# A short table for v in PSUM, one reciprocal per half batch, two batches' hypermixer in one pass, more buffers and a new order

## The chip, the cores and the metric

The kernel runs on one core of one Trainium2 chip. The metric is the device time of one launch in microseconds (us). TensorE is called PE in the profile (PEld is its weight load), VectorE DVE, ScalarE ACT, GpSimd POOL, SyncE SP; SP issues all transfers. A core has 16 DMA engines.

## What is computed

Linear attention with cosine weights, then a token mixer, over 8 batches of 576 tokens, 8 heads of 64:

```python
r = relu(x);  phi(x) = concat([r * cos_w, r * sin_w], -1)    # cos_w, sin_w: one number per position
kv  = einsum('bhsf,bhsd->bhfd', phi(k), v);  z = sum(phi(k), axis=2)
x   = (phi(q) @ kv) / (phi(q) . z + 1e-6)                    # heads side by side: [8, 576, 512]
wq, wk = x @ w_q, x @ w_k                                    # 64 columns each
mixed  = (wq @ wk^T / 8) @ x                                 # over the tokens of one batch
out    = relu(mixed) @ w_out                                 # [8, 576, 512] float32
```

q, k and v are float32 in HBM, 9.4 MB each; out is 9.4 MB. The kernel works in bfloat16 and sums in float32.

## The kernel before, in words

The work is cut into 16 half batches H (four heads each, two pairs of heads side by side in the 128 partitions), 8 batches b, and for the last product 36 row tiles of 128 tokens. Every piece of work is a *step*, a small Python function that issues the instructions of one piece. The string `ORDER` (L24) names all steps with their index, the PSUM bank or bank pair that they write (`:4`) and the engine (`@A` ACT, `@V` DVE, `@G` POOL). The loop at L434 issues them in just this order, so each engine's program is `ORDER` cut to its steps. No scheduler moves anything; an engine waits at its next instruction until the operands are there and the buffer is free.

The steps of one half batch:

- `LK LQ LV` (L129) load k, q, v: two DMAs of 288 KB each, on SP's queue, into raw buffers (`NRAW` = 4 per tensor).
- `RK`, `RQ` (relu, L201, L204) and `CV` (a cast of v, L208) make bfloat16 of them, on ACT or POOL.
- `VS` (L211, DVE) multiplies v by cosine and by sine of the position. The table `vtab` (L137) holds both for each of 9 positions, repeated 64 times along the head's columns: 1152 bfloat16 a partition in SBUF.
- `QT` (L239, PE) transposes q in 18 small transposes; `QM` (L252, DVE) multiplies the result, out of PSUM, by `qtab`.
- `KV` (L227, PE) makes kv and z in 36 matmuls; `KE` (L248) copies them to SBUF.
- `N` (L261, PE), twice per half batch (index g = 2H + r): 20 matmuls that make numerator and denominator.
- `EP` (L274, ACT or DVE) adds eps to 10 denominators a partition; `X` (L281, DVE) takes their reciprocal (L286) and multiplies 640 numerators a partition by it (L287). Both once per g, so 32 times.
- `XT` or `XR` (L292, L303, PE) transpose x; `XE` copies that to SBUF.

Then for each batch: `WK KW WQ QW` (wk, wq and their copies out of PSUM), `KX XK` (wk^T x), `XA XB` (copy halves of it across partitions), four `MX` (two matmuls each, L378) with `ME` (relu, L388); and for two batches at a time nine row tiles `WO` (four matmuls of 512 columns, L398), `OE` (copy) and `ST` (store, L412), out of `NOUT` = 12 output buffers. PSUM has eight banks of 2 KB a partition; `pair(i)` is banks i and i + 1. `make_identity`, iotas (`TK`, `TQ`) and ACT's `Sin` (`TV`, `TW`, `T2`) make identity and tables at the start; `LW`, `CW` load and cast the weights.

Of the kernel before, what the change touches and what calls it, by code (L numbers as in the profile page):

```python
# [24 lines left out]
LV1 LQ0b LQ1 TK CV1@G TQ LK1 TV LV0a TI TZ LV0b T2 RK1@G RQ1@A TW VS1 LK0a CV0b@A QT1:0 RQ0b@A  # L25
LQ0a CV0a@G KV1:2 LK0b RK0a@G RQ0a@A QM1 KE1@V RK0b@A VS0a VS0b N2:4 LV3 LQ3 RQ3@A LK3 CV3@G EP2@V
N3:6 LV2 LK2 QT0:0 KV0:2 X2 EP3@A LQ2 RK3@G QM0 KE0@A VS3 N0:4 LV5 X3 QT3:0 EP0@A KV3:2 QM3 LW0
LW1 X0 CV2@G KE3@A RK2@A VS2 XT1:6 N1:0 EP1@A LK5 LQ4 X1 N6:4 CV5@G LQ5 XE1@A RQ2@A EP6@A LV7 N7:2
LV4 KV2:0 QT2:6 EP7@A LQ7 KE2@V XT0:0 X6 CW1 QM2 CW0 N5:4 XE0@A WK0:6 N4:0 RK5@A X7 RQ5@G WQ0:7
VS5 EP4@V X4 EP5@V KW0@A RQ4@A KX0:6 XR3:2 XK0@A QW0@V X5 XB0@A XE3@A XA0@A KV5:0 LK4 LQ6 KE5@A  # L30
QT5:6 LW2 XT2:4 CV7@G MX1:2 QM5 LV6 XE2@A MX3:0 QT4:6 CV4@G ME1@A ME3@A RK4@G MX2:4 VS4 LK7 QM4
WK1:2 WQ1:3 KW1@A N11:0 RQ7@G KX1:2 CW3@G N10:6 QW1@V ME2@A MX0:4 XK1@A EP11@A ME0@A VS7 X11 KV4:2
EP10@A KE4@A N9:4 X10 N8:0 RQ6@A CW4@G XT5:2 EP8@A X8 LV8 LK6 CV6@G RK7@G QT7:6 LV10 CW2@A EP9@A
X9 XA1@A CW5@A WO1:0 XE5@A LQ8 LV9 XR4:4 QT6:2 WO2:1 QM7 OE1:0@A KV7:6 XB1@G QM6 RK6@G VS6 XE4@A
MX7:2 WQ2:0 KE7@A MX4:4 ME7@A OE2:1@A N15:6 MX5:2 QW2@A ME4@V EP15@A WK2:1 N14:4 LK10 ME5@A KW2@A
KV6:2 EP14@A X15 CV8@G KE6@A MX6:0 ME6@A KX2:6 LQ9 X14 N12:2 VS8 LK8 XK2@A EP12@A N13:0 EP13@A X13
# [12 lines left out]
WK5:5 ME19@A X24 MX18:0 N27:6 XR12:2 OE14:8@A KW5@A ST5 ME18@A VS15 RQ15@G EP27@A RK15@G N26:4
KX5:0 XK5@A EP26@V WO18:1 WO16:0 X27 X26 QT15:6 QT14:4 XE12@A OE16:7@A XR13:2 WO20:0 OE18:6@A ST8  # L50
RK14@G VS14 XE13@A QM14 WO19:1 QM15 ST7 WK6:2 OE20:5@A XB5@A KV15:4 XA5@G KW6@A KV14:6 ST20 MX23:2
OE19:4@V KE15@A MX21:0 ST0 WQ6:4 ME21@A KE14@V KX6:5 ME23@V MX20:0 N30:6 MX22:2 QW6@V WO21:4
ME20@A N29:0 EP30@V ST2 ME22@A XK6@A N28:2 X30 N31:6 EP29@A EP28@A X29 X28 OE21:11@A ST12 XB6@A
WO24:5 XA6@G WO22:4 OE24:2@A WO23:5 EP31@A X31 OE22:5@A XR14:0 XR15:2 XE14@A MX27:6 OE23:3@V
WO25:4 ST18 XE15@V ST16 WK7:5 ME27@V OE25:1@A MX26:0 KW7@A ME26@A MX25:2 ST14 MX24:6 WQ7:4 KX7:5
ME24@V ME25@A WO26:0 XK7@A QW7@V XB7@A WO29:1 MX31:6 XA7@G ST22 MX28:2 ME31@A ST9 MX30:4 OE26:10@V
WO28:0 ST21 MX29:6 ST23 ST1 ME30@A OE29:6@V WO30:1 ST25 ME29@A ST19 ME28@V ST29 OE28:7@V WO32:0
ST24 WO31:4 ST26 ST28 WO33:5 OE32:8@V OE30:5@A ST32 ST30 OE31:9@A ST31 OE33:11@A WO27:6 OE27:3@A
ST33 WO35:7 ST27 OE35:0@A ST35 WO34:2 OE34:1@A ST34
# [4 lines left out]
def kernel(  # L64
# [29 lines left out]
    NRAW, NPREP, NV2, NQM, NX, NXT, NOUT = (4, 2, 2, 2, 2, 2, 12)  # L94
# [41 lines left out]
    qi = pool.tile([P, 2, C, H2], I32, name="qi")  # L136
    vtab = pool.tile([P, C, 2, D], BF16, name="vtab")  # L137
# [5 lines left out]
    wo_f = pool.tile([P, NDM, DM], FP32, name="wof")  # L143
    wqw = pool.tile([P, NDM, DH], BF16, name="wqw")
# [8 lines left out]

    def TV(i, ps, eng):
        nc.scalar.activation(vtab, ki.unsqueeze(3).to_broadcast([P, C, 2, D]),
                             AF.Sin, bias=0.0, scale=coef)

# [10 lines left out]
    def T2(i, ps, eng):  # L168
        for b in v2_b:
            for pr in range(2):  # L170
                nc.scalar.activation(b[:, pr, :, :, D:DV],
                                     ki.unsqueeze(3).to_broadcast([P, C, 2, 2]),
                                     AF.Sin, bias=0.0, scale=coef)

    def TZ(i, ps, eng):
        for b in qm_b:
            nc.gpsimd.memset(b[:, :, :, C, :], 0.0)
        for b in xT_b:
            nc.gpsimd.memset(b[:, :, C, :], 0.0)
        nc.gpsimd.memset(eps_t, EPS)  # L180
# [30 lines left out]
    def VS(H, ps, eng, part):  # L211
        n = part.stop - part.start
        V.tensor_mul(  # L213
            v2_b[H % NV2][:, part, :, :, 0:D],
            vb_b[H % NPREP][:, part].unsqueeze(3).to_broadcast([P, n, C, 2, D]),
            vtab.unsqueeze(1).to_broadcast([P, n, C, 2, D]))
# [22 lines left out]
    def QT(H, ps, eng):  # L239
        place["QT", H] = ps  # L240
        qt_v = qt_view(ps)
        for c in range(C):
            for r in range(2):
                a = slice(H2 * r, H2 * r + H2)
                nc.tensor.transpose(qt_v[:, r, c * H2:(c + 1) * H2],  # L245
                                    rq_b[H % NPREP][a, c, :, :], ident[a, a])

    def KE(H, ps, eng):  # L248
        cast(eng, kv_b[H % 2][:, :, :, 0:D + 1],
             kv_view(place["KV", H]).rearrange("p r (s e) -> p r s e", s=2))  # L250

    def QM(H, ps, eng):  # L252
        V.tensor_mul(  # L253
            qm_b[H % NQM][:, :, :, 0:C, :].rearrange("p s r c d -> p s r (c d)"),
            qt_view(place["QT", H]).unsqueeze(1).to_broadcast([P, 2, 2, S]),
            qtab.rearrange("p s c d -> p s (c d)").unsqueeze(2).to_broadcast([P, 2, 2, S]))
# [4 lines left out]
    def N(g, ps, eng):  # L261
# [3 lines left out]
        for u in range(SC):  # L265
            for s in range(2):
                for pr in range(2):
                    a = slice(H2 * pr, H2 * pr + H2)
                    nc.tensor.matmul(  # L269
                        nv[:, pr, u, :], qm_b[H % NQM][a, s, r, 2 * u:2 * u + 2, :],  # L270
                        kv_b[H % 2][a, r, s, 0:D + 1],
                        start=(u == 0 and s == 0), stop=(u == SC - 1 and s == 1))

    def EP(g, ps, eng):  # L274
        den = num(place["N", g])[:, :, :, D:D + 1]
        if eng is A:
            A.activation(rec_b[g % 8], den, AF.Identity, bias=eps_t)  # L277
        else:
            V.tensor_scalar(rec_b[g % 8], den, EPS, None, op0=ALU.add)

    def X(g, ps, eng):  # L281
        H, r = divmod(g, 2)
        b, h = divmod(H, 2)
        rec = rec_b[g % 8]
        nv = num(place["N", g])
        V.reciprocal(rec, rec)  # L286
# [3 lines left out]
            nv[:, :, :, 0:D], rec.to_broadcast([P, 2, SC, D]), op=ALU.mult)  # L290
# [46 lines left out]
    def KW(b, ps, eng):  # L337
        cast(eng, wk_b[b % 2], bank(place["WK", b])[:, 0:SC * DH].rearrange(
# [15 lines left out]

    def KX(b, ps, eng):
        place["KX", b] = ps
        o = bank(ps)
        for u in range(SC):
            for t in range(2):
                nc.tensor.matmul(  # L360
                    o[H2 * t:H2 * t + H2, 0:XC], wk_b[b % 2][:, u, :],
# [15 lines left out]

    def MX(i, ps, eng):  # L378
# [9 lines left out]
    def ME(i, ps, eng):  # L388
# [4 lines left out]
        if eng is A:  # L393
            A.activation(dst, s, AF.Relu, scale=scale_moe)  # L394
        else:
            V.tensor_scalar(dst, s, scale_moe, 0.0, op0=ALU.mult, op1=ALU.max)
# [18 lines left out]
    def LW(i, ps, eng):  # L415
# [14 lines left out]
    steps = {f.__name__: f for f in (KV, QT, KE, QM, N, EP, X, XT, XR, XE, WK, KW, WQ, QW, KX, XK, XA, XB,  # L430
                                     MX, ME, WO, OE, ST, LW, CW, TK, TV, TI, TQ, TW, T2, TZ)}
# [46 lines left out]
```

## Time and profile before

| what | value |
|---|---|
| median of 3 runs | 123.55 us (123.04 to 128.03) |
| span of the profiled execution, first to last instruction | 120.7 us; the median is 2.85 us longer, what lies around the span |
| busy | PE 94.8, DVE 88.2, ACT 84.2, POOL 52.2 us |
| moved | 39.40 MB, mean 326 GB/s; read 29.62 MB, written 9.44 MB |
| granted TensorE clock | 0.991 |

The page's chart cuts the span in 40 slices of 3 us; a digit is the busy share in tenths. The *windows* view gives each engine's busy time in a stretch. The *groups* list instructions of one line with their mean duration; the *timeline* gives start and duration of single ones, with the idle time before and what ended it in brackets. In the *chain of waits* a line is start, duration and what ran; a row there is the time from one group's turn to the next one's, so it leaves out the overlap that a duration of the groups holds.

### The profile page before, as it was taken

What the parts mean: (1) busy time and instruction counts of PE and PEld (TensorE: products, weight loads), DVE (VectorE), ACT (ScalarE), POOL (GpSimd) and SP (SyncE); (2) the same over time, 40 slices, a digit from 0 to 9 for tenths busy, and PEclk for the clock granted to TensorE, in tenths of its full rate; (3) what the DMA queues carried; (4) which work ended last, traced back from release to release, by engine and by line L of the source; (5) the groups of instructions that cost most, each with busy time, mean ns of one, the idle gap of its engine ahead of it and who ended that gap; (6) DMA issues with size and microseconds to landing.
All of it is one profiled execution on the core that took longest, in us unless ns stands there. A gap on an engine that the chain in (4) does not pass through costs nothing.

```text
span 120.7 us, 5301 instructions
## 1 busy us (share of the span) xinstructions
PE 94.8 (79%) x2286; PEld 63.1 (52%) x2286; DVE 88.2 (73%) x132; ACT 84.2 (70%) x155; POOL 52.2 (43%) x63
## 2 busy tenths in 40 slices
PE   0005919758778899969999999798999999999950
PEld 0004818637656656635667576454755864653410
DVE  0136998889989998997979987759969868766200
ACT  7246452967887989777967897586678668757450
POOL 2577136032739758146799304937365310010000
PEclk9999999999999999999999999999999999999996
DMA  3999999999999999999989999999997681875685
GB/s 111 318 384 405 395 391 391 361 405 396 392 390 408 398 337 344 355 360 379 383 282 326 364 285 391 343 331 283 391 299 263 238 329 55 320 288 198 237 331 196
DMA packets 20615, 39.40 MB, mean 326 GB/s; under 512 B 3184, under 2 KB 3184, under 8 KB 20592
## 3 DMA queue, kind: packets, MB, share of 16 engines
q1 hardware_dynamic: 20592, 39.07, 89.8%
q8 instruction: 18, 0.29, 1.0%
q14 instruction: 5, 0.04, 0.1%
HBM read 29.62 MB, written 9.44 MB: 324 GB/s over the span
## 4 chain that ended last, share of the span: by engine, by line
DMA 39%; PE 39%; DVE 6%; issue 4%; SPq 3%; ACT 3%; POOL 2%; DVEq 0%; ACTq 0%; POOLq 0%
DMA kraw<-in_k_dram 24%; PE ps L403 20%; DMA vraw<-in_v_dram 11%; DMA out_dram<-o 5%; PE ps L234 3%; PE ps L383 3%; PE ps L269 3%; SPq L132 3%; PE ps L360 3%; DVE v L213 2%; PE ps L313 2%; DVE x L287 2%; PE ps L245 2%; PE ps L333 2%; PE ps L346 2%
## 5 line engine op out<-in xcount | busy, mean ns | idle before, releaser
L403 PE MATMUL ps<-wow,mix 128*128 128x512 bf16 x144 | 34.7, 380 | 0.0
L287 DVE TENSOR_TENSOR x<-ps,rec 128x640 bf16<-128x640 f32 x32 | 26.4, 824 | 2.2
L195 POOL TENSOR_SCALAR vb<-vraw 128x1152 bf16<-128x1152 f32 (+1 forms) x16 | 17.9, 1122 | 20.9 <-DMA vraw<-in_v_dram 18.6
L213 DVE TENSOR_TENSOR v<-vb,vtab 128x2304 bf16<-128x2304 bf16 (+1 forms) x17 | 21.7, 1289 | 6.6 <-POOL vb L195 6.6
L253 DVE TENSOR_TENSOR qm<-ps,qtab 128x2304 bf16<-128x2304 bf16 x16 | 21.4, 1350 | 4.6 <-ACT qtab L166 2.9
L193 ACT COPY o<-ps 128x512 f32<-128x512 f32 x30 | 17.5, 587 | 6.6 <-PE ps L403 4.5
L269 PE MATMUL ps<-kvs,qm 64*128 64x65 bf16 x640 | 15.3, 199 | 6.0 <-ACT kvs L193 3.3
L403 PEld LDWEIGHTS <-mix 128*128 128x128 bf16 x144 | 12.4, 98 | 14.2 <-issue 0.9
L394 ACT ACTIVATE mix<-ps 128x576 bf16<-128x576 f32 x26 | 16.4, 657 | 3.2 <-PE ps L383 3.2
L189 POOL TENSOR_SCALAR rq<-qraw 128x1152 bf16<-128x1152 f32 x9 | 13.4, 1487 | 11.4 <-DMA qraw<-in_q_dram 10.8
L269 PEld LDWEIGHTS <-qm 64*128 64x128 bf16 x640 | 13.3, 100 | 9.4 <-issue 5.7
L189 POOL TENSOR_SCALAR rk<-kraw 128x1152 bf16<-128x1152 f32 (+1 forms) x12 | 13.8, 1150 | 9.4 <-DMA kraw<-in_k_dram 7.0
L193 ACT COPY xT<-ps 128x1280 bf16<-128x1280 bf16 (+1 forms) x13 | 15.4, 1186 | 3.3 <-PE ps L313 1.7
L234 PE MATMUL ps<-v,rk 64*64 64x130 bf16 x576 | 12.5, 236 | 3.0 <-DVE x L287 1.3
L245 PE MATMUL ps<-ident,rq 64*128 64x64 bf16 x288 | 7.6, 199 | 9.3 <-ACT rq L187 8.8
L187 ACT ACTIVATE rq<-qraw 128x1152 bf16<-128x1152 f32 (+1 forms) x8 | 8.4, 1046 | 6.6 <-DMA qraw<-in_q_dram 6.6
L234 PEld LDWEIGHTS <-rk 64*64 64x64 bf16 x576 | 10.1, 117 | 5.2 <-ACT rk L187 1.4
L245 PEld LDWEIGHTS <-rq 64*128 64x128 bf16 x288 | 6.1, 101 | 11.7 <-ACT rq L187 9.0
L383 PE MATMUL ps<-wq,kx 64*128 64x288 bf16 x64 | 8.3, 287 | 0.3 <-ACT xT L193 0.2
L195 POOL TENSOR_SCALAR kx<-kx 64x256 bf16<-64x256 bf16 x7 | 2.8, 399 | 12.6 <-ACT kx L193 12.2
L286 DVE RECIPROCAL rec<-rec 128x10 f32<-128x10 f32 x32 | 6.8, 211 | 1.8 <-ACT rec L277 1.4
L277 ACT ACTIVATE rec<-ps,eps 128x10 f32<-128x10 f32 x23 | 6.2, 273 | 1.7 <-PE ps L269 1.6
(46 smaller groups left out, 99.3 us busy)
## 6 DMA issues: line engine op xcount, KB each, us to landing
vraw<-in_v_dram SPq DMA_DIRECT2D x32, 288.0 KB, 6.0
qraw<-in_q_dram SPq DMA_DIRECT2D x32, 288.0 KB, 5.9
kraw<-in_k_dram SPq DMA_DIRECT2D x32, 288.0 KB, 5.9
out_dram<-o SPq DMA_DIRECT2D x36, 256.0 KB, 3.1
wof<-in_moe_w_out_dram SPq DMA_DIRECT2D x1, 1024.0 KB, 7.6
wqf<-in_moe_w_q_dram SPq DMA_DIRECT2D x1, 128.0 KB, 5.5
wkf<-in_moe_w_k_dram SPq DMA_DIRECT2D x1, 128.0 KB, 5.2
```

What stands on the lines that cost most here:

```text
L189: eng.tensor_scalar(dst, s, FMAX, 0.0, op0=ALU.min, op1=ALU.max)
L193: A.copy(dst, s)
L195: G.tensor_scalar(dst, s, 1.0, 1.0, op0=ALU.mult, op1=ALU.mult)
L213: V.tensor_mul(v2_b[H % NV2][:, part, :, :, 0:D], vb_b[H % NPREP][:, part].unsqueeze(3).to_broadcast([P, n, C, 2, D]), vtab.unsqueeze(1).t ...
L234: nc.tensor.matmul(kv_v[o, r, :], rk_b[H % NPREP][a, pr, c, :], v2_b[H % NV2][a, pr, c, :, 0:D + 1], start=(c == 0), stop=(c == C - 1))
L245: nc.tensor.transpose(qt_v[:, r, c * H2:(c + 1) * H2], rq_b[H % NPREP][a, c, :, :], ident[a, a])
L253: V.tensor_mul(qm_b[H % NQM][:, :, :, 0:C, :].rearrange("p s r c d -> p s r (c d)"), qt_view(place["QT", H]).unsqueeze(1).to_broadcast([P, ...
L269: nc.tensor.matmul(nv[:, pr, u, :], qm_b[H % NQM][a, s, r, 2 * u:2 * u + 2, :], kv_b[H % 2][a, r, s, 0:D + 1], start=(u == 0 and s == 0), ...
L287: V.tensor_tensor(x_b[b % NX][:, :, 4 * h:4 * h + 4, :].rearrange("p u (w r) d -> p r w u d", r=2)[:, r], nv[:, :, :, 0:D], rec.to_broadca ...
L383: nc.tensor.matmul(pair(ps)[:, t, :].bitcast(FP32)[:, 0:HS], kx_b[b % 2][a, (m // 2) ^ t, (m % 2) * P:(m % 2 + 1) * P], wq_b[b % 2][a, :], ...
L394: A.activation(dst, s, AF.Relu, scale=scale_moe)
L403: nc.tensor.matmul(o, mix_b[bp % 2][:, m, rt * P:(rt + 1) * P], wow[:, m, :], start=(m == 0), stop=(m == NDM - 1))
```

## The change

- **Table for v.** `vtab` shrinks from 1152 to 72 bfloat16 a partition: each number twice instead of 64 times (and all of it twice over, for both pairs of heads). `TP`, on DVE, copies it to the last 144 bytes of PSUM bank 7, and `VS` on DVE reads it there, with a step of 0 over the 32 pairs of a head's columns. `T2` is now two copies of this table on DVE. No `WO` uses bank 7 any more.
- **VS on POOL.** For H = 3, 7, 9, 11, 12, 14 and 15 `VS` stands on POOL: two products, cosine and sine, straight from the float32 raw v, without the cast `CV`.
- **Joint eps and reciprocal.** `EP` becomes `EJ` and the reciprocal `RC`, once per half batch over 20 numbers; `X` keeps only its product.
- **Two batches in one pass**, for batches 4 and 5: `WP QP KP XP MP MM` do the work of `WQ QW KX XK MX ME` with batch 4 in the lower and batch 5 in the upper 64 partitions, and without `XA`, `XB`. The other six batches keep the old steps.
- **Whole transposes.** `QU` (9 transposes of 128 columns in place of 18 of 64) with a `QM` in two instructions, for H = 5, 8, 9 and 11.
- **Buffers.** Raw 4 to 5 per tensor, output 12 to 16, kv and wk 2 to 3; `rec` from 8 small ones to 4 large. The integers `qi` lie in the weight buffer `wo_f` until `LW` loads it, now in four parts.
- **ORDER** is new from the first to the last step, and the halves of a load are placed one by one. The step `XJ` is defined and not used.

```diff
-    NRAW, NPREP, NV2, NQM, NX, NXT, NOUT = (4, 2, 2, 2, 2, 2, 12)
+    NRAW, NPREP, NV2, NQM, NKV, NX, NXT, NWK, NOUT = (5, 2, 2, 2, 3, 2, 2, 3, 16)
-LV1 LQ0b LQ1 TK CV1@G TQ LK1 TV LV0a TI TZ LV0b T2 RK1@G RQ1@A TW VS1 LK0a CV0b@A QT1:0 RQ0b@A
+LQ1b LV1a LV1b LK1a LK1b LV0b LQ1a RK1a@A LQ0b LQ0a CV1a@G LV0a TI RQ1b@A TQ TK TV CV1b@A RQ1a@A
...
-    vtab = pool.tile([P, C, 2, D], BF16, name="vtab")
+    vtab = pool.tile([P, 2 * C, 2, 2], BF16, name="vtab")
+    vt_ps = PS[:, 7, 2048 - 16 * C:2048].bitcast(FP32)
+    def TP(i, ps, eng):
+        nc.vector.tensor_copy(vt_ps, vtab.rearrange("p x s e -> p (x s e)").bitcast(FP32))
...
     def VS(H, ps, eng, part):
+        if eng is G:
+            v = raw["v"][H % NRAW][:, part].rearrange("p r (c d) -> p (r c) d", d=D)
+            for s in range(2):
+                G.tensor_tensor(o[:, :, :, s].rearrange("p r c d -> p (r c) d"), v,
+                                vtab[:, 0:n * C, s, 0:1].to_broadcast([P, n * C, D]), op=ALU.mult)
+            return
         V.tensor_mul(
-            vb_b[H % NPREP][:, part].unsqueeze(3).to_broadcast([P, n, C, 2, D]),
-            vtab.unsqueeze(1).to_broadcast([P, n, C, 2, D]))
+            vb_b[H % NPREP][:, part].rearrange("p r c (h e) -> p (r c) h e", e=2).unsqueeze(2)
+            .to_broadcast([P, n * C, 2, D // 2, 2]),
+            vt_v[:, 0:n * C].unsqueeze(3).to_broadcast([P, n * C, 2, D // 2, 2]))
...
-    def EP(g, ps, eng):
-        den = num(place["N", g])[:, :, :, D:D + 1]
+    def EJ(H, ps, eng):
+        den = both(H)[0][:, :, :, :, D:D + 1]
+    def RC(H, ps, eng):
+        V.reciprocal(rec_b[H % 4], rec_b[H % 4])
     def X(g, ps, eng):
-        V.reciprocal(rec, rec)
...
+    def KP(p, ps, eng):
+        for u in range(SC):
+            for j in range(2):
+                nc.tensor.matmul(
+                    bank(ps)[H2 * j:H2 * j + H2, :], wk_b[(2 * p + j) % NWK][:, u, :],
+                    x_b[(2 * p + j) % NX][:, u].rearrange("p h d -> p (h d)"),
+                    start=(u == 0), stop=(u == SC - 1))
```

ACT's program at its start (rk, rq: relu of k and q; vb: cast of v; rec: eps). Before:

```order
L155 ACT_TABLE_LOAD
L155 ACTIVATE vtab<-ki 128x1152
L171 ACTIVATE v_81<-ki 128x18x2 x2
L171 ACTIVATE v_82<-ki 128x18x2 x2
L187 ACTIVATE rq_78<-qraw_68 128x2x9x64
L166 ACTIVATE qtab<-qi 128x1152
```

and now:

```order
L198 ACT_TABLE_LOAD
L198 ACTIVATE rk_79<-kraw_64 128x576
L198 ACTIVATE rq_81<-qraw_69 128x9x64
L165 ACT_TABLE_LOAD
L165 ACTIVATE vtab<-ki 128x72
L204 CAST vb_83<-vraw_74 128x576
L198 ACTIVATE rq_81<-qraw_69 128x9x64
L180 ACTIVATE qtab<-wof 128x1152
```

The tables, which stood ahead of the first loaded data, now stand behind k's and q's first halves, and a second table load stands ahead of them.

DVE's program behind its first QM (qm, for H = 1) up to the end of X for H = 0. Before, with one EP, reciprocal and product per g:

```order
L197 CAST kvs_86<-ps 128x4x65
L213 TENSOR_TENSOR v_81<-vb_79,vtab 128x18x64 x2
L279 TENSOR_SCALAR rec_89<-ps 128x10
L286 RECIPROCAL rec_89<-rec_89 128x10
L287 TENSOR_TENSOR x_95<-ps,rec_89 128x2x5x64
L253 TENSOR_TENSOR qm_83<-ps,qtab 128x4x576
L213 TENSOR_TENSOR v_82<-vb_80,vtab 128x36x64
L286 RECIPROCAL rec_90<-rec_90 128x10
L287 TENSOR_TENSOR x_95<-ps,rec_90 128x2x5x64
L253 TENSOR_TENSOR qm_84<-ps,qtab 128x4x576
L286 RECIPROCAL rec_87<-rec_87 128x10
L287 TENSOR_TENSOR x_95<-ps,rec_87 128x2x5x64
```

and now:

```order
L231 TENSOR_TENSOR v_84<-vb_82,ps 128x18x64 x2
L286 TENSOR_TENSOR qm_86<-ps,qtab 128x4x576
L318 TENSOR_SCALAR rec_92<-ps 128x20
L321 RECIPROCAL rec_92<-rec_92 128x20
L327 TENSOR_TENSOR x_95<-ps,rec_92 128x2x5x64 x2
L318 TENSOR_SCALAR rec_91<-ps 128x20
L321 RECIPROCAL rec_91<-rec_91 128x20
L327 TENSOR_TENSOR x_95<-ps,rec_91 128x2x5x64 x2
```

VS and QM for H = 3, which stood between the X products of H = 1 and H = 0, are gone from here: VS to POOL, QM behind them.

POOL's program from its first relu of q (H = 0) on, now:

```order
L200 TENSOR_SCALAR rq_80<-qraw_68 128x9x64 x2
L200 TENSOR_SCALAR rk_78<-kraw_63 128x576
L228 TENSOR_TENSOR v_85<-vraw_76,vtab 128x18x64 x2
L206 TENSOR_SCALAR vb_82<-vraw_75 128x1152
L206 TENSOR_SCALAR wkw<-wkf 128x256
L206 TENSOR_SCALAR vb_82<-vraw_77 128x1152
```

The third row is the product for H = 3 in two instructions. Before, POOL had only casts and relus of one input here.

195 lines of the change are left out of this document (130 added, 65 removed).

## The prediction

> **What bounds the kernel now.** I read the page's sums and chart first, then the windows, then the timeline of the start and the chain.
>
> ```profile
> PE 94.8 (79%) x2286; PEld 63.1 (52%) x2286; DVE 88.2 (73%) x132; ACT 84.2 (70%) x155; POOL 52.2 (43%) x63
> PE   0005919758778899969999999798999999999950
> DVE  0136998889989998997979987759969868766200
> ```
>
> PE has the most work, but its row is full only from about the middle on; before that DVE's row is the fuller one. The windows put numbers on it:
>
> ```profile
> 8.80:42.00 33.20, 23.83 (x728) 19.88 (x729) 29.05 (x46) 23.56 (x42) 16.18 (x15) 1.00 1.06 394
> 42.00:116.40 74.40, 70.94 (x1559) 43.25 (x1557) 57.81 (x86) 55.90 (x108) 31.57 (x31) 1.00 0.87 307
> 116.40:120.70 4.30, 0.00 (x0) 0.00 (x0) 0.00 (x0) 0.55 (x1) 0.00 (x0) 0.75 0.68 254
> ```
>
> The columns are PE, PEld, DVE, ACT, POOL, clock, DMA share, GB/s. From 8.8 to 42 us DVE is busy 29.05 of 33.2 us (88%), and the loads come at 394 GB/s; PE waits. From 42 to 116.4 us PE is busy 70.94 of 74.4 us (95.4%), whatever the others do. The last 4.3 us are one copy and the last store. So the time is three terms: **when DVE has handed over enough** (about 42 us), **PE's remaining work divided by its share** (74.4), **the end** (4.3): 120.7. What lies around the span, 2.85 us to the median, I add unchanged.
>
> DVE's early part runs from its first QM to the product for the 12th g, which ends where the last row here starts:
>
> ```profile
> 9.83 1.36 DVE L253 TENSOR_TENSOR qm<-ps,qtab 128x2304 bf16<-128x2304 bf16 x1 [2.88 <-ACT qtab L166]
> ...
> 38.29 0.21 DVE L286 RECIPROCAL rec<-rec 128x10 f32<-128x10 f32 x1
> 38.60 0.82 DVE L287 TENSOR_TENSOR x<-ps,rec 128x640 bf16<-128x640 f32 x1
> 39.34 0.20 DVE L286 RECIPROCAL rec<-rec 128x10 f32<-128x10 f32 x1
> ...
> 42.43 2.63 DVE L253 TENSOR_TENSOR qm<-ps,qtab 128x2304 bf16<-128x2304 bf16 x2
> ```
>
> These starts also give what an instruction costs in a row of others: reciprocal to product 0.31, product to the next 0.74, a QM 1.28 (2.63 for two, less the overlap).
>
> **The start.** By the order, ACT now does k's first half, q's first half, a second table load, the small table, a cast, q's other half, then qtab; QM for H = 1 needs qtab. The rows:
>
> ```profile
> 0.73 1.28 ACT L155 ACT_TABLE_LOAD   x1 [0.73 <-PEq L462]
> 7.58 1.16 ACT L187 ACTIVATE rq<-qraw 128x1152 bf16<-128x1152 f32 x1 [3.90 <-DMA qraw<-in_q_dram]
> 8.65 1.15 ACT L166 ACTIVATE qtab<-qi 128x1152 bf16<-128x1152 int32 x1
> 10.76 0.67 ACT L193 CAST vb<-vraw 128x576 bf16<-128x576 f32 x1 [0.96 <-DMA vraw<-in_v_dram]
> 11.33 0.68 ACT L187 ACTIVATE rq<-qraw 128x576 bf16<-128x576 f32 x1
> ...
> 4.41 1.15 POOL L195 TENSOR_SCALAR vb<-vraw 128x1152 bf16<-128x1152 f32 x1 [3.08 <-DMA vraw<-in_v_dram]
> ```
>
> The second load had landed by 4.41 and the fifth by 7.58, so the fourth (k's first half now) lands at about 6.6. A half costs 0.57 in a row (10.76 to 11.33). 6.6 + 0.57 + 0.57 + 1.28 + 0.2 + 0.57 + 0.6 + 1.15 = 11.5, so QM starts at about 11.6, 1.8 us later than at 9.83. On this path the second table load alone costs 1.28; before, the only one was over at 2.0, hidden by the first loads. VS for H = 1 and KV fit into the wait.
>
> **DVE's early part.** The durations:
>
> ```profile
> L287 DVE TENSOR_TENSOR x<-ps,rec 128x640 bf16<-128x640 f32 x32 | 26.4, 824 | 2.2
> L253 DVE TENSOR_TENSOR qm<-ps,qtab 128x2304 bf16<-128x2304 bf16 x16 | 21.4, 1350 | 4.6 <-ACT qtab L166 2.9 <-PE ps L245 1.7
> L213 DVE TENSOR_TENSOR v<-vb,vtab 128x2304 bf16<-128x2304 bf16 x15 | 20.2, 1350 | 6.6 <-POOL vb L195 6.6
> L197 DVE COPY o<-ps 128x512 f32<-128x512 f32 x6 | 4.1, 688 | 2.6 <-PE ps L403 2.4
> L197 DVE COPY xT<-ps 128x1280 bf16<-128x1280 bf16 x3 | 2.5, 817 | 0.0
> L213 DVE TENSOR_TENSOR v<-vb,vtab 128x1152 bf16<-128x1152 bf16 x2 | 1.6, 830 | 0.0
> L279 DVE TENSOR_SCALAR rec<-ps 128x10 f32<-128x10 f32 x9 | 1.5, 163 | 2.3 <-ACT mix L394 1.2 <-PE ps L269 1.2
> ```
>
> *VS with its table in PSUM* no row shows. From below, 1.35, as QM, which reads bfloat16 of the same size out of PSUM. From above, one element per cycle: 640 take 0.824 and 512 take 0.688 from PSUM, 1.06 ns each, so 0.824 + 1664 x 1.06 ns = 2.59 us. I take 1.35: QM is the nearest in every respect but the step of 0. [...]
>
> In the new order DVE does, from that QM to the 12th product: five QM (6.4), one QM in two pieces (1.5), VS for H = 0 in halves (1.5) and for 2, 4, 5 (3.8), six times EJ 0.2, RC 0.31 and two products 1.48 (11.9), three copies of xT (0.74 each, 2.2) and one of wk (0.4, between the rows for 512 and 10 elements). Sum 27.7; from 11.6 that is 39.3. Idle time on top: before, 33.2 - 29.05 = 4.1 in that stretch, 1.0 of it ahead of QM, so 3.1; bounds 0 and 3.1, I take 1.6: **40.9** against 42.4. The savings (VS for 3 and 7 off DVE 2.5, six reciprocals and some eps less 2) are half eaten by the late start and the copies.
>
> **VS on POOL.** No row shows a product there.
>
> ```profile
> L195 POOL TENSOR_SCALAR vb<-vraw 128x1152 bf16<-128x1152 f32 x15 | 17.2, 1152 | 20.8 <-DMA vraw<-in_v_dram 18.6 <-DVE qm L253 2.0
> ...
> 37.02 2.35 POOL L189 TENSOR_SCALAR rq<-qraw 128x1152 bf16<-128x1152 f32 x1
> 55.27 1.15 POOL L189 TENSOR_SCALAR rq<-qraw 128x1152 bf16<-128x1152 f32 x1 [2.54 <-DMA qraw<-in_q_dram]
> ...
> 37.02 1.35 DVE L213 TENSOR_TENSOR v<-vb,vtab 128x2304 bf16<-128x2304 bf16 x1
> ```
>
> With one input 1152 elements take 1.15; two inputs cost between that and double, 2.3, so a VS 2.3 to 4.6 and seven 16 to 32 us; the seven casts that fall away give 8.1 back. I take the upper end, since a second input is a second read. POOL then has some 65 us of work in 117, and the products have room: H = 7's v, 48 half loads into the queue, lands by about 39 at 394 GB/s, and PE reaches its KV some 10 us of work after DVE's 40.9, at about 51. [...]
>
> The last three rows show what the table in PSUM is worth to POOL: a relu beside a VS took 2.35, alone 1.15, so POOL stands still while DVE's VS has both inputs in SBUF. With nine VS left on DVE that is at most 9 x 1.35 = 12 us, on an engine that is idle more than half the time: nothing for the end.
>
> **PE's rest.** What PE pays per step, from the chain:
>
> ```profile
> 40.53 0.73 PE ps L300 x10
> 45.45 0.61 PE ps L346 x8
> 46.06 0.23 PE ps L383 x2
> 49.89 0.73 PE ps L269 x40
> 50.62 0.97 PE ps L403 x4
> 58.13 0.65 PE ps L234 x34
> 58.78 0.69 PE ps L333 x20
> 60.35 0.67 PE ps L360 x10
> 91.09 0.63 PE ps L245 x36
> 91.72 0.29 PE ps L313 x20
> 110.17 6.17 PE ps L403 x28
> ```
>
> So KV 0.65, QT 0.3, N 0.36, XT 0.7, XR 0.36 (0.29 when nothing holds it), WK 0.67, WQ 0.61, KX 0.6, MX 0.23, WO 0.93 (between 0.97 and 6.17 / 7 = 0.88). All of before's steps together are 90.1; those behind its first WO, 71.0, against 70.94 in the window, so the prices hold. In the change PE stands behind its first two WO and eight MX when the 12th product ends. Left are 10 KV (6.5), 10 QT or QU (3.0, the nine large ones at the price of 18 small), 20 N (7.2), XT and 10 XR (4.3), 6 WK (4.0), 6 WQ and 6 KX (7.3; the joint pass issues the same columns, so it saves PE nothing), 24 MX (5.5), 34 WO (31.6): **69.4**, 1.6 less than before had left at 42.
>
> PE's share: 95.4% before. DVE's sum changes little: seven VS (-9.5) and 16 reciprocals (-3.4) go; six copies of xT (+4.9), three of the output (+2.1) and others come, about -2. ACT sheds more:
>
> ```profile
> L193 ACT COPY xT<-ps 128x1280 bf16<-128x1280 bf16 x8 | 9.8, 1229 | 1.7 <-PE ps L313 1.7
> ```
>
> Six such copies are 7.4, and 20 EP of at least 0.16 another 3.3, besides a dozen copies under 0.7 each; five relus of 1.16 and the table load take 7.1 back. Between 90 and 98% of PE's share the groups settle nothing; its 3.5 us of waits should shrink a little with an emptier ACT: I take 96%, so 69.4 / 0.96 = **72.3**. The joint pass (it saves ACT and POOL the four copies across and two casts) counts in that.
>
> **At nothing:** raw buffers, output buffers and the moved stores. PE is full from 42 on whatever lands when; two stores fewer ahead of the last load are worth 0.5 MB / 394 GB/s = 1.3 us of a load that PE does not wait for. If PE were done sooner they would count. The end stays one copy and one store: 4.3.
>
> **Sum:** 40.9 + 72.3 + 4.3 = 117.5, and 2.85 around it: **120.4 us**, 2.6% under the median of 123.55. About 2% is what a measurement of this kernel can tell from no change.
>
> **Rivals.** *The waits stay* (0.30): DVE idles its 3.1 as before and PE's share is between 95.4 and 92%, since each product now waits for both N of its half batch and holds four banks of PSUM instead of two, and WO has lost bank 7. For it: QM's row shows 1.7 us of DVE waiting for PE even now; against: ACT is emptier. 42.4 + 72.7 to 75.4 + 4.3 + 2.85 = 122.3 to 125.0.
>
> *The order fits better* (0.20): almost no idle time on DVE (0.5) and PE at 98%: 39.8 + 70.8 + 4.3 + 2.85 = 117.8. For it: five raw buffers let loads run ahead, and freed engines have slack; against: PE is at 95% already.
>
> *VS loses its pace* (0.12), the slower one: with the table in PSUM read pair by pair, VS runs one element per cycle, 2.59. Five VS stand ahead of the 12th product, 5 x 1.24 = 6.2 later, and four more (5.0) in PE's stretch, which take PE's share to 95%: 47.1 + 73.1 + 4.3 + 2.85 = 127.3. It decides from about 2.45 us per VS on, where five times the excess is 5.6 us, the 3.1 of gain and the 2%.
>
> That the change does not do what it says can be left out: the order shows its counts.
>
> **How the numbers follow.** Forecast 0.38, rivals 0.30, 0.20, 0.12. Under 121.1 lie two thirds of the forecast, all of the second rival and a little of the first: faster 0.53. Over 126.0 lie most of the third and a tail of the first: slower 0.13. The rest, 0.34, is within 2%. The range takes in the second rival and most of the third: 115.8 to 126.5; the forecast's own is 118.5 to 122.
>
> **What would show it.** Right: VS on DVE near 1.35 and none of POOL's relus at 2.35; the first QM near 11.6 behind a second table load; the 12th product near 41; PE at 96% from there to the last WO; the span near 117.5. Wrong: VS at 2.5; a VS on POOL that PE or DVE waits for; PE's share under 94% with DVE or bank waits in front of N, XT or WO.

## The result and the profile after

The changed kernel takes 132.57 us (median of 4 runs, 130.98 to 133.58) beside 124.66 us for the kernel before on the same chip: a ratio of 1.071, 95% interval 1.058 to 1.084. It is slower, and by more than the prediction's range allowed. The profiled execution took 133.1 us, its span 131.3 us; the forecast had a span of 117.5. The executions of a kernel fall into a faster and a slower state: the medians here are over all of them, a ratio compares the faster ones alone (so it is not the quotient of the medians), and the profile of the changed kernel is of a slower one.

The page's sums and three rows of its chart (a slice is 3.28 us):

```profile
PE 97.2 (74%) x2237; PEld 65.0 (49%) x2250; DVE 86.6 (66%) x134; ACT 75.2 (57%) x121; POOL 64.0 (49%) x65
...
PE   0005864797777779979997686099979999999980
...
PEclk9999999559999999999999999756999999999999
DMA  4999999999999999999999999920000828609695
```

No engine has much more work than forecast; the engines stand still longer. PE's row, full behind the middle before, now has a hole (686099), and twice TensorE's granted clock is one half (0.50 from 22.45 to 29.28 us and from 83.89 to 90.72). The windows, cut where the prediction cut them:

```profile
12.29:47.19 34.90, 25.07 (x700) 19.31 (x693) 27.63 (x41) 18.46 (x30) 21.01 (x22) 0.90 1.06 383
47.19:127.70 80.51, 71.12 (x1513) 44.71 (x1525) 56.65 (x85) 49.86 (x84) 37.45 (x27) 0.96 0.72 268
127.70:131.30 3.60, 0.00 (x0) 0.00 (x0) 0.00 (x0) 0.57 (x1) 0.00 (x0) 1.00 0.60 224
```

The first row runs from the first QM to the end of the 12th product, the second to the end of PE's work. Put beside the prediction's three terms:

| term | predicted | measured | where the difference lies |
|---|---|---|---|
| first QM | 11.6 | 12.29 | +0.7 |
| DVE up to the 12th product: work, idle | 27.7 + 1.6 | 27.63 + 7.27 | idle +5.7 |
| PE's rest: work, idle | 69.4 + 2.9 | 71.12 + 9.39 | work +1.7, idle +6.5 (share 88%, not 96%) |
| end | 4.3 | 3.60 | -0.7 |
| span | 117.5 | 131.3 | +13.8 |

Both sums of work came within 3%; both estimates of waiting were wrong. What was priced piece by piece, from the groups:

```profile
L231 DVE TENSOR_TENSOR v<-vb,ps 128x2304 bf16<-128x2304 bf16 x7 | 9.4, 1347 | 1.2 <-ACT wqp L204 1.0 <-POOL vb L206 0.2
L228 POOL TENSOR_TENSOR v<-vraw,vtab 128x1152 bf16<-128x1152 f32 x14 | 29.5, 2129 | 15.2 <-issue 12.8 <-DMA vraw<-in_v_dram 2.4
L200 POOL TENSOR_SCALAR rq<-qraw 128x1152 bf16<-128x1152 f32 x5 | 5.7, 1146 | 0.2
```

VS reads its table out of PSUM at 1347 ns, a product on POOL costs 2129, and POOL's relus of 1152 elements take 1146: none stands still beside a VS any more. Now the waits. DVE's timeline in its early part, the rows with idle time ahead of them (in brackets, with the releaser):

```profile
25.20 0.18 DVE L318 TENSOR_SCALAR rec<-ps 128x20 f32<-128x20 f32 x1 [0.87 <-PE ps L302]
29.73 0.18 DVE L318 TENSOR_SCALAR rec<-ps 128x20 f32<-128x20 f32 x1 [0.90 <-PE ps L302]
38.65 0.18 DVE L318 TENSOR_SCALAR rec<-ps 128x20 f32<-128x20 f32 x1 [0.94 <-PE ps L481]
45.11 0.18 DVE L318 TENSOR_SCALAR rec<-ps 128x20 f32<-128x20 f32 x1 [2.19 <-PE ps L498]
```

DVE waits for PE at the joint eps. The last is odd: L498 is WO, which eps does not read. And PE in its turn:

```profile
34.23 0.42 PE L264 MATMUL ps<-ident,rq 64*128 64x64 bf16 x17 [0.82 <-DVE v L231]
...
37.76 0.78 PE L302 MATMUL ps<-kvs,qm 64*128 64x65 bf16 x39 [0.90 <-DVE v L231]
...
78.29 1.02 PE L498 MATMUL ps<-wow,mix 128*128 128x512 bf16 x4
...
80.48 0.57 PE L302 MATMUL ps<-kvs,qm 64*128 64x65 bf16 x26
85.17 0.56 PE L302 MATMUL ps<-kvs,qm 64*128 64x65 bf16 x14 [4.12 <-issue]
...
88.43 1.90 PE L498 MATMUL ps<-wow,mix 128*128 128x512 bf16 x4
```

Three things to see. QT stops after 1 of its 18 transposes and N after 1 of 40 matmuls, for DVE's VS, whose result neither uses. N stops for 4.12 us after 26 of 40, and nothing is named ("issue"). Behind that stop the same WO takes 1.90 in place of 1.02.

Four causes offer themselves, and each can be undone alone. **A**: the table lies in PSUM bank 7, and a step that writes bank 7 waits for the VS that reads it (the stops of 0.82 and 0.90 us). **B**: PE's instructions come late (the 4.12 us in N). **G**: the clock falls behind a thinly filled stretch (0.50 from 83.89 us on, in that stop). **J**: the joint eps waits for more than it reads (the 2.19 us that end with WO). Rivals: the products on POOL, the second table load, the joint pass, the depth of the loads.

### The profile page after: what moved, and what is told of

Read it like the earlier page. It is cut to its first block, busy times and chain, and to the rows that moved or that the text cites. A ratio compares the mean times of both kernels' runs of the same rounds, so it can differ in the third digit from the quotient of the medians.

```text
span 131.3 us, 5171 instructions
## 1 busy us (share of the span) xinstructions
PE 97.2 (74%) x2237; PEld 65.0 (49%) x2250; DVE 86.6 (66%) x134; ACT 75.2 (57%) x121; POOL 64.0 (49%) x65
## 4 chain that ended last, share of the span: by engine, by line
PE 55%; DVE 16%; DMA 14%; issue 7%; ACT 2%; SPq 2%; POOL 1%; DVEq 0%; POOLq 0%
PE ps L498 23%; DMA vraw<-in_v_dram 10%; PE ps L302 7%; DVE v L231 5%; PE ps L253 5%; DMA qraw<-in_q_dram 5%; PE ps L383 4%; DVE x L327 4%; PE ps L363 3%; DVE qm L286 2%; PE ps L452 2%; PE ps L481 2%; PE ps L264 2%; PE ps L396 2%; SPq L137 2%
## 5 line engine op out<-in xcount | busy, mean ns | idle before, releaser
L228 POOL TENSOR_TENSOR v<-vraw,vtab 128x1152 bf16<-128x1152 f32 x14 | 29.5, 2129 | 15.2 <-issue 12.8
L498 PE MATMUL ps<-wow,mix 128*128 128x512 bf16 x131 | 34.6, 393 | 1.2 <-issue 0.7
L302 PE MATMUL ps<-kvs,qm 64*128 64x65 bf16 x640 | 15.7, 200 | 10.1 <-issue 5.9
L498 PEld LDWEIGHTS <-mix 128*128 128x128 bf16 x144 | 12.9, 100 | 15.0 <-issue 1.9
L302 PEld LDWEIGHTS <-qm 64*128 64x128 bf16 x640 | 13.2, 100 | 12.5 <-issue 9.7
L286 DVE TENSOR_TENSOR qm<-ps,qtab 128x2304 bf16<-128x2304 bf16 x12 | 16.0, 1353 | 3.8 <-PE ps L264 2.9
L206 POOL TENSOR_SCALAR vb<-vraw 128x1152 bf16<-128x1152 f32 (+1 forms) x9 | 9.4, 1044 | 10.6 <-DMA vraw<-in_v_dram 10.3
L231 DVE TENSOR_TENSOR v<-vb,ps 128x2304 bf16<-128x2304 bf16 (+1 forms) x11 | 12.2, 1128 | 1.2 <-ACT wqp L204 1.0
L198 ACT ACTIVATE rk<-kraw 128x1152 bf16<-128x1152 f32 (+1 forms) x8 | 8.3, 1042 | 7.0 <-DMA kraw<-in_k_dram 7.0
L198 ACT ACTIVATE rq<-qraw 128x1152 bf16<-128x1152 f32 (+1 forms) x11 | 11.8, 1076 | 0.4 <-DMA qraw<-in_q_dram 0.4
L204 ACT CAST kvs<-ps 128x260 bf16<-128x260 f32 x13 | 4.9, 378 | 10.8 <-PE ps L253 10.7
L200 POOL TENSOR_SCALAR rk<-kraw 128x1152 bf16<-128x1152 f32 (+1 forms) x10 | 10.5, 1050 | 1.2 <-DMA kraw<-in_k_dram 0.8
L204 ACT COPY xT<-ps 128x1280 bf16<-128x1280 bf16 (+1 forms) x7 | 8.3, 1190 | 2.9 <-PE ps L363 2.8
L318 DVE TENSOR_SCALAR rec<-ps 128x20 f32<-128x20 f32 x13 | 2.3, 174 | 11.3 <-PE ps L302 6.7
```

What stands on the lines that cost most here:

```text
L198: A.activation(dst, s, AF.Relu)
L204: A.copy(dst, s)
L206: G.tensor_scalar(dst, s, 1.0, 1.0, op0=ALU.mult, op1=ALU.mult)
L228: G.tensor_tensor(o[:, :, :, s].rearrange("p r c d -> p (r c) d"), v, vtab[:, 0:n * C, s, 0:1].to_broadcast([P, n * C, D]), op=ALU.mult)
L231: V.tensor_mul(o.rearrange("p r c s (h e) -> p (r c) s h e", e=2), vb_b[H % NPREP][:, part].rearrange("p r c (h e) -> p (r c) h e", e=2).u ...
L286: V.tensor_mul(qm_b[H % NQM][:, :, :, 0:C, :].rearrange("p s r c d -> p s r (c d)"), qt_view(at).unsqueeze(1).to_broadcast([P, 2, 2, S]), ...
```

## The experiments

All times are medians; beside them stands the ratio to the kernel before on the same chip, with its interval. A gain or loss in us is a difference of two such medians, and by the intervals it is uncertain by one to two us.

**Table read in SBUF.**

```
-            vt_v[:, 0:n * C].unsqueeze(3).to_broadcast([P, n * C, 2, D // 2, 2]))
+            vtab[:, 0:n * C].unsqueeze(3).to_broadcast([P, n * C, 2, D // 2, 2]))
```

> The changed kernel, but VS on DVE reads the short table in SBUF; the copy in PSUM bank 7 is made and read by nobody. Theory A (a step that writes bank 7 has to wait for the VS that reads the table there and stands ahead of it in the order): PE's five stops in the middle of QT, KV and N that DVE's VS ends (0.79 + 0.82 + 0.90 + 0.67 + 0.87 = 4.05 us) go, and the time falls from 132.6 to about 128.5, a ratio to before of 1.03. Rival (these stops are only where PE would have waited anyway, for the same VS at its KV or for products): the stops move to the next KV and the time stays within 1.5 us of 132.6, ratio 1.06 to 1.075. VS itself should stay at 1.35 us by both, and some relus on POOL go back to 2.3 us.

129.80 us, 1.041 (1.030 to 1.052). The stops inside QT, N and KV for H = 12 are gone; part comes back at a KV, which needs the other operands too:

```profile
34.54 0.72 PE L253 MATMUL ps<-v,rk 64*64 64x130 bf16 x36 [1.28 <-POOL rk L200]
```

That one waits for POOL, whose relus are slower again, 1347 against 1146:

```profile
L200 POOL TENSOR_SCALAR rq<-qraw 128x1152 bf16<-128x1152 f32 x5 | 6.7, 1347 | 0.2
```

From the first QM to the end of the 12th product it is 32.84 us, 2.1 less than the changed kernel's 34.90 (that length is compared from here on, since the first QM itself comes up to 1 us earlier or later from run to run). In the four profiles in which no edit bears on this stretch (the changed kernel, and below fewer instructions, two batches one by one, half of the loads) it is 34.4 to 35.4. So A holds, for 2.8 us of the 4.05 expected, and the two intervals stand apart.

**Sine table first.**

```
-... RQ1b@A TQ TK TV CV1b@A ...
+TK TV LQ1b LV1a LV1b ...   (first words of the order)
```

> The changed kernel, but the iota and the sine table for v stand first on POOL and ACT, ahead of the first loaded data, so ACT needs only one table load. Theory D (the start is on the path that sets the end): first QM 1.3 us earlier (11.0 in place of 12.3) and the time 1 to 1.3 us shorter, 131.4. Rival: DVE waits in its early part for loads and for PE anyway, so that the first QM is earlier and the time within 0.5 us of 132.6.

131.84 us, 1.051 (1.036 to 1.066). One table load is left, and the first QM starts at 10.83, 1.46 us earlier:

```profile
10.83 1.36 DVE L286 TENSOR_TENSOR qm<-ps,qtab 128x2304 bf16<-128x2304 bf16 x1 [1.36 <-ACT qtab L180]
```

DVE waits some 0.7 us more behind it (35.69 to the 12th product, little outside that spread), and the time is 0.7 less: too small against the intervals to tell theory from rival.

**Fewer instructions on PE.**

```
-XR8:6 XR10:0 XR11:2 QT10:0 QT12:4 QT13:6
+XT8:6 XT10:0 XT11:2 QU10:0 QU12:4 QU13:6
```

> The changed kernel, but six steps in the dense stretch use whole transposes: XR becomes XT for H = 8, 10, 11 and QT becomes QU for H = 10, 12, 13: some 114 PE instructions fewer (weight loads and matmuls), the same work. Theory B (PE's instructions arrive in pieces of 256, and PE stands still where the next piece is not there): the stops at the ends of pieces, 1.2 us at 74.65 and 4.1 us at 81.05, leave their steps in the middle of N and stand 60 to 114 instructions later in the program, again 256 apart, and as more time passes per piece they shrink by 2 us or more; the time falls by 2 to 5 us (the half clock after the long stop may go too). Rival (PE waits there for something else, PSUM or a product): the 4.1 us stop stays in the middle of N for g = 22 or 23 and the time within 1 us of 132.6.

127.69 us, 1.025 (1.017 to 1.032): 4.9 us less for *more* TensorE time. In the place of the two long stops stand these:

```profile
78.40 0.82 PE L498 MATMUL ps<-wow,mix 128*128 128x512 bf16 x3 [0.90 <-issue]
...
84.89 0.44 PE L383 MATMUL ps<-wkw,xT 128*128 128x64 bf16 x9 [0.41 <-issue]
```

They stand in other steps (WO, WK), but at the same place counted in PE's instructions: in seven runs (table in SBUF, sine first, this one, four raw buffers, two batches one by one, eps apart, half loads) PE stops after 2753 and after 3009 of them, 256 apart, whatever step that is. The transfers of 16384 bytes each, 17 of them in the changed kernel's profile on a queue of their own that the page calls `q8 instruction`, fit to that (a piece is one such transfer; times in us, worked out from the trace's records of transfers and instructions; "out of instructions" is the end of the last matmul):

```
kernel      PE enters    next piece       PE out of       PE goes
            a piece      is transferred   instructions    on
before      47.86        50.50 to 51.42   51.95           52.96
changed     70.47        73.49 to 74.53   74.65           75.84
changed     75.84        82.69 to 83.73   81.05           85.17
fewer       78.40        82.46 to 83.34   84.48           84.89
```

These pieces begin 2.6 to 6.9 us after PE enters the one before, take 0.9 to 1.0, and PE needs 1.3 to 1.6 more. In all 16 profiles together PE has 41 stops of over 0.3 us for which nothing is named, and each ends 1.2 to 1.6 us after such a transfer does. Where 256 instructions are KV, XR and N, they are used up sooner: in the changed kernel 36 matmuls of KV took 0.72 us (at 79.24), 40 of XR 0.76 and 26 of N 0.57, where four of WO took 1.02. B is shown.

**Table in SBUF, and all VS on DVE.**

```
-VS3@G  (so for 7, 9, 11, 12, 14, 15)
+CV3@G VS3@V
```

> As the run with the table in SBUF, and besides VS for H = 3, 7, 9, 11, 12, 14, 15 on DVE with its cast on POOL, as before the change; so order, joint steps and buffers are new and all of VS is old. Theory C (the products on POOL, 4.2 us per VS in one queue with relus and copies across, hold KV back): 2 us or more faster than the run with the table in SBUF. Rival (POOL's products have room, DVE's 9.4 us more do not): 2 us or more slower than it, since DVE's 12th product comes one VS later and DVE is fuller. If both small, within 1 us of it, and the slowdown lies in the order itself.

134.51 us, 1.080 (1.074 to 1.087): 4.7 us slower than the first experiment. From the first QM to the 12th product it is 35.94 us, 3.1 more. So the products on POOL are a gain.

**Three edits together** (table in SBUF, sine first, fewer instructions).

> Three edits together on the changed kernel: VS's table in SBUF, the sine table first, and the whole transposes for H = 8, 10, 11 (x) and 10, 12, 13 (q). If the three causes are separate, their single gains of 2.8, 0.7 and 4.9 us add up: 132.6 - 8.4 = 124.2, level with before. Rival (the same wait paid only once, so that what one removes the other cannot): no better than 127, the best of the three alone.

125.95 us, 1.015 (1.000 to 1.029): 6.6 of 8.4, and under the rival's 127. Most of the gains add up.

**Four raw buffers.**

```
-    NRAW, NPREP, NV2, NQM, NKV, NX, NXT, NWK, NOUT = (5, 2, 2, 2, 3, 2, 2, 3, 16)
+    NRAW, NPREP, NV2, NQM, NKV, NX, NXT, NWK, NOUT = (4, 2, 2, 2, 3, 2, 2, 3, 16)
```

> The changed kernel with four raw buffers per tensor in place of five (nine half loads stand later in the order for that). Theory F (loads that run ahead keep the DMA engines at 390 GB/s up to 85 us, and PE's next piece of instructions comes late because of it): the DMA engines are less full between 60 and 85 us, the delay of those pieces falls from 5 to 8 us to under 4, the stop of 4.1 us in N shrinks by 2 us or more, and the time falls to 128 to 130.5 although loads come later. Rival (the delay has nothing to do with the loads' depth): stop and delay stay, the time is 132 to 135, as loads come later and nothing else changes.

130.93 us, 1.055 (1.045 to 1.064). The stop in N shrinks from 4.12 to 2.74, but the one before it grows from 1.19 to 2.00, and the late piece still comes 5.55 us after PE enters the one before, though the transfers run at 222 GB/s in that stretch in place of 406. Between theory and rival, and the intervals overlap.

**Whole transposes early.**

```
-QT2:0 QT3:6
+QU2:0 QU3:6
```

> The changed kernel with whole transposes of q for H = 2 and 3: more TensorE time (some 0.3 us each) and 0.15 us more for each QM on DVE, nothing taken away. Theory G (the clock falls to half when matmuls were busy less than half of one 3.41 us window; in the changed kernel the window from 19.0 to 22.4 us holds 0.49): the window rises over one half, no half clock from 22 to 29 us, and the 12th product ends 1 to 3 us earlier in spite of the added work; time 130 to 131.5. Rival (the clock falls for another reason, or DVE alone sets this stretch): half clock as before, 12th product 0.3 us later, time 132.6 to 133.2.

128.57 us, 1.038 (1.029 to 1.048): 4.0 us less by adding work, but not as expected. The windows fell otherwise in this run and half clock came twice for 3.4 us in place of once for 6.8, and up to the 12th product it is 34.70 us, as good as unchanged. The gain came from the ends of pieces, which moved by 36 instructions: the stops of 1.19 and 4.12 became none and 2.09, and the half clock behind the second lasted 3.4 us in place of 6.8. So this run speaks for B, and G's forecast of it failed.

All profiles together do better for G. The records of the granted clock last 6.83, 54.61 and 40.96 us in the changed kernel's trace and 95.57 in that of the kernel before (but for the last of each), whole multiples of 3.41. I cut each profile in windows of 3.41 us from its first clock record and took the share in which matmuls ran. Of windows at full clock, 25 had under 0.50: the next window had half the clock in 25 of 25. From 0.50 to 0.60 it was 5 of 20, above 0.60 none of some 400. (Windows at the end of PE's work are left out.) Full clock came back after a half-clock window of 0.86 or more (30 of 30), and not after one of 0.81 or less (15 of 15). The changed kernel has 0.49 from 19.0 and, because of the stop in N, 0.17 from 80.5; the lowest of the kernel before, 0.57, stood not far above, and its next window kept full clock. What half clock costs this kernel no run shows apart from the other causes.

**Two batches one by one.**

```
-WP2:6 QP2@A ... KP2:4 XP2@A ... MP18:4 ... MM16@V ...
+WQ4:6 QW4@A WQ5:7 QW5@A ... KX4:4 XK4@A XA4@G XB4@G KX5:5 XK5@A XA5@G XB5@G ... MX16:4 ... ME17@V ...
```

> The changed kernel with batches 4 and 5 mixed one by one by the old steps, in the places of the joint ones (two copies across each on POOL more, banks 6, 7, 4, 5 for the four products). Theory: the joint pass saves PE nothing and the others little, so within 1 us of 132.6. Rival H (the joint pass is what holds PE between 88 and 97 us, since it needs both batches before it starts): 1.5 us or more faster; rival I (it saved real waits for the copies across): 1.5 us or more slower.

134.15 us, 1.075 (1.064 to 1.086). That is 1.6 us slower, by the number just rival I's, but the two intervals overlap almost wholly. (WO for row tile 23 stands ahead of the last relu of its batch here and multiplies older columns in its place; the work is the same.) Rival H is out: the joint pass is not what costs the time.

**Four edits** (the three, and whole transposes early).

> The three edits of the combined run and the whole transposes of q for H = 2 and 3: 186 instructions on PE fewer than the changed kernel. If the gain of those two transposes (4.0 us alone) is the early half clock and later stops at ends of pieces, part of it is used up by the other edits: a further 1 to 3 us, time 123 to 125, level with before (124.8). Rival (it is all the same gain by fewer instructions): no better than 125.5.

123.17 us beside 124.47, ratio 1.004 (0.995 to 1.012): level with before, as expected. (The edits take 150 instructions off PE, 4350 in place of 4500; the 186 above is a wrong sum.) PE's share behind the 12th product is back at 97%.

**Four edits, still wider** (XT also for H = 9, 12, 13).

> As the run before it, and whole transposes of x for H = 9, 12 and 13 too: 60 instructions fewer and some 0.8 us more TensorE time. Theory B: a stop at the end of a piece of 0.8 us or more that is left goes, and the time is 0 to 1 us shorter. Rival (no such stop is left worth it): 0.5 to 1 us longer.

124.02 us, 1.014 (1.003 to 1.024): 0.85 us longer, as the rival has it, though the intervals overlap. No gain is seen from the last stops.

**The kernel before with whole transposes** (XT in place of XR for H = 7, 9, 10, 11).

> The kernel before the change with whole transposes of x for H = 7, 9, 10 and 11: 80 instructions fewer on PE, some 1.1 us more TensorE time, nothing else. Theory B in the other kernel: its stops at ends of pieces (1.20, 0.44, 0.54 and 0.59 us at 51.8, 67.8, 79.2 and 84.0 us) shrink by 2 us or more in sum, and the time falls by 1 us, ratio 0.99. Rival (PE's time is what counts there): 1 us longer, ratio 1.01.

125.56 us, 1.018 (0.984 to 1.052). No gain is seen, in a wide interval: the stops are 0.52, 1.32, 0.53 and 1.60 us now, at other places, and this profile has half clock early (from 17.9 and from 24.7) and behind the stop of 1.32, which the one of before has not. Fewer instructions shift all later ends of pieces, and it seems that where these fall counts as much as their number; it can't be aimed by counting alone.

**Eps apart.** For H = 5 the two N lie in bank pairs 0 and 4. The program's wait shows what J says: eps waits for PE's 721st matmul (the end of the second WO, in bank 2, which lies between the two) and not for the 711th (N's last).

```
-            V.tensor_scalar(rec_b[H % 4], den, EPS, None, op0=ALU.add)
+            for j, at in enumerate(sorted((place["N", 2 * H], place["N", 2 * H + 1]))):
+                V.tensor_scalar(rec_b[H % 4][:, j], num(at)[:, :, :, D:D + 1], EPS, None,
+                                op0=ALU.add)
```

> The changed kernel, but eps is added in two instructions of ten numbers where the two N of a half batch lie in pairs of banks that are not neighbours (H = 2, 5, 14). Theory J (the joint eps names its two pairs by a stride, and everything between them counts as read: for H = 5 it waits for PE's 721st matmul, the second WO, in place of the 711th, the end of N): that eps starts at 43.2 in place of 45.1, the 12th product ends 1.9 us earlier, at 45.3, and the time falls by 1 to 2 us. Rival (DVE or PE meets the same wait one step later): the 12th product less than 0.7 us earlier, the time within 0.7 us of 132.6.

129.82 us, 1.052 (1.043 to 1.062), 2.75 us less.

```profile
41.56 0.15 DVE L319 TENSOR_SCALAR rec<-ps 128x10 f32<-128x10 f32 x1
41.88 0.17 DVE L319 TENSOR_SCALAR rec<-ps 128x10 f32<-128x10 f32 x1 [0.16 <-PE ps L302]
42.08 0.28 DVE L325 RECIPROCAL rec<-rec 128x20 f32<-128x20 f32 x1
42.39 1.55 DVE L331 TENSOR_TENSOR x<-ps,rec 128x640 bf16<-128x640 f32 x2
```

It waits for N (L302) now, and up to the 12th product it is 32.65 us, 2.25 less: J holds. The intervals of the time (to 1.062, and from 1.058) just overlap; the next run settles that. (Here and in the next run eps is apart for H = 2 and 14 too, whose pairs are not neighbours either.)

**All five edits.**

> The best kernel so far (table in SBUF, sine first, eight steps of whole transposes; 123.2) with eps in two instructions as in the run before. Theory J: 12th product at 42.6 in place of 44.6, and since PE has no long stop left behind it, all of it reaches the end: 121.3, 2.5% under the kernel before the change. Rival: the gain is lost again on PE, whose share behind the 12th product falls below 96%: 122.5 to 123.5.

120.92 us beside 124.22, ratio 0.983 (0.976 to 0.989): faster than the changed kernel, and 1.7% under the kernel before, clear of 1 but not of the 2% that the prediction took as its limit. From the run with four edits (0.995 to 1.012) it differs in the eps alone, and these intervals stand apart, so here J's gain is clear of noise.

```profile
10.74:41.31 30.57, 23.89 (x681) 18.46 (x673) 28.14 (x45) 17.85 (x28) 21.75 (x21) 0.94 1.06 384
41.31:115.10 73.79, 70.39 (x1470) 44.44 (x1468) 57.94 (x89) 50.42 (x84) 43.14 (x29) 1.00 0.86 320
115.10:118.80 3.70, 0.00 (x0) 0.00 (x0) 0.00 (x0) 0.58 (x1) 0.00 (x0) 1.00 0.60 225
```

Up to the 12th product it is 30.57 us with DVE idle for 2.43, PE at 95.4% behind it, span 118.8. The rival's sign is there (a share under 96%), its time is not. The span lies near the forecast's 117.5, but that proves none of the forecast's terms: this is another kernel, without the table in PSUM and with one table load.

**Half of the loads left out.**

```
-... LK11b ... LV11b ... LQ11b ...   (and for H = 12, 13, 14)
```

> The changed kernel without the second halves of the loads of k, q and v for H = 11 to 14 (12 loads, 3.5 MB); the steps work on what an earlier half batch left in these buffers, so all work on the engines stays. Theory F (PE's pieces of instructions come late because the transfers of data stand ahead of them): where the DMA engines are less busy the pieces begin under 1.5 us after the piece before them is entered, as they do behind 86 us now (0.0 to 1.0 us), the stop of 4.1 us in N and the half clock behind it go, and the time falls by 4 us or more, to 128 or less. Rival (delay of PE's own making): delays of 4 to 7 us and the stop stay, whatever the transfers do.

131.38 us, 1.055 (1.041 to 1.070). The stop stays, and the clock behind it:

```profile
83.90 0.56 PE L302 MATMUL ps<-kvs,qm 64*128 64x65 bf16 x14 [3.29 <-issue]
84.39 1.89 PE L498 MATMUL ps<-wow,mix 128*128 128x512 bf16 x4
```

So the theory failed as it was put. Where the transfers were thinner, at 283 to 314 GB/s, three pieces came 0.68, 4.38 and 2.44 us after PE entered the one before, which is no clear gain; and the late one (6.19 us) fell where they were full again, at 376 GB/s. What does hold, in the changed kernel as here: behind the last load the next four pieces come after 0.0 to 1.1 us, and under stores at some 380 GB/s after 2.2 or 2.3. So the pieces came later under full stores than behind the last load. Why this one comes after 5.4 to 7 us in nine of the profiles, where most come after 2 to 4 under the same load, stays open.

## Why the prediction was wrong

- *"VS with its table in PSUM ... I take 1.35"*: right, 1.347, and the rival that it loses its pace is out. The step that failed is beside it: the table was priced as an operand only. As a tenant of bank 7 it ties QT, N and KV to DVE's order (A, 2.8 us).
- *"QM starts at about 11.6"*: 12.29, by the terms named. Right mechanism, 0.7 short: ACT began on k's first half at 7.23, not 6.6, and what follows took as long as summed. Without the second table load the end is 0.7 earlier, no more than the noise.
- *DVE's early part*: work 27.63 against 27.7. **"Bounds 0 and 3.1, I take 1.6" failed**: 7.27. The bound was the idle time of the order before, and it says nothing about another order. The runs put A (2.1 less without it) and J (2.25 less) in its place, and with both undone, in the run with all five edits, 2.43 us of idle time are left. The half clock from 22.5 to 29.3 stood in the same stretch; what it added was not measured.
- *VS on POOL, 2.3 to 4.6 us per half batch*: 4.3 (two products of 2129 ns). "The products have room" held: putting them back costs 4.7 us.
- *PE's rest*: 71.12 of work against 69.4; half clock is in it. **"I take 96%" failed**: 88%. Of the 9.39 us of idle time in place of 2.9, the three stops at ends of pieces (0.62, 1.19 and 4.12 us) are 5.9 and two waits for VS (A) 1.5. The forecast had no term for a late piece of instructions. In the run with four edits the share is 97%, in that with five 95.4%, so 96% was within reach of this order, but not in the kernel as it was changed. The timeline of the kernel before has such a stop too, in the middle of an XR, and it was passed over:

```profile
51.52 0.43 PE L313 MATMUL ps<-ident,x 64*128 64x64 bf16 x17
52.96 0.23 PE L313 MATMUL ps<-ident,x 64*128 64x64 bf16 x3 [1.01 <-issue]
```

- *"The joint pass issues the same columns, saves PE nothing"*: no run speaks against it (1.6 us slower without it, within the intervals; its share of the work was not measured apart).
- *At nothing: raw buffers and moved stores.* Put at nothing because PE doesn't wait for loads. It doesn't, but the pieces of instructions came later under full stores (2.2 or 2.3 us after PE entered the one before) than behind the last load (0.0 to 1.1). Four buffers in place of five changed the stops (4.12 to 2.74, 1.19 to 2.00); the 1.6 us less is within the intervals, so what the fifth buffer costs stays open.
- *The rival "the waits stay"* was the right direction and stopped at 125.0: it kept before's 3.1 us on DVE and let PE's share fall no lower than 92%.

The single gains (2.8, 0.7, 4.9, 4.0, 2.75) sum to 15.1, all five edits together give 11.7. It may be that 4.9 and 4.0 overlap, both being fewer instructions, but with one to two us of uncertainty on each gain this is not shown.

## What to carry to other kernels

When all work is put in a new order, sums of work can be forecast from the old profile to a few per cent, but its waits are no bound for the new ones: ask of each step what its operand's *bank* and its access's whole extent tie it to. Where PE stops in the middle of a step and the profile names only "issue", look whether the stops stand 256 instructions apart, as they do behind 2753 and 3009 in seven runs here: there it was a late piece of instructions, and moving instructions moved the stop. Half clock came behind all 25 windows at full clock that matmuls filled to less than 0.50, and behind 5 of the 20 filled to 0.50 to 0.60; the kernel before the change, with 0.57 in its lowest, stood next to such a step.

## What the runs showed of the hardware

- PE stopped for up to 4.12 us (changed kernel, up to 85.17) with nothing named, in seven runs at two places 256 of its instructions apart; each of the 41 such stops of over 0.3 us in the 16 profiles ended 1.2 to 1.6 us after a transfer of 16384 bytes on the queue `q8 instruction`.
- In the 16 profiles half clock followed each of the 25 windows of 3.41 us at full clock with matmuls in under 0.50 of it, 5 of 20 from 0.50 to 0.60 and none of some 400 above 0.60. It ended behind each of the 30 windows at half clock that were 0.86 full or more, and behind none of the 15 at 0.81 or less.
- On DVE a product with one operand read out of PSUM with a step of 0 took 1347 ns for 2304 bfloat16 (VS, changed kernel), against 1353 for QM in the same run and 1350 for VS with both operands in SBUF (kernel before).
- ACT loaded one table where the sine comes first (at 0.73 us in the run with the sine table first) and two where relu does (at 0.73 and 8.51, changed kernel), 1.28 us each.
